# Seven products instead of eight in the last eight-product layer, and two partial sums seeded in PSUM, in a linear attention and two-layer feed-forward kernel

## The chip, the cores and the metric

The kernel runs on one NeuronCore of a Trainium2 chip. The metric is the device time of one execution in microseconds (us). Before the change it is 1583.31 us, the median of three runs (1581.37 to 1585.13).

## The reference, cut to what matters

```python
kv = einsum('bhsd,bhse->bhde', k, v)            # 8 batches, 8 heads, 576 tokens, 64 wide
out = einsum('bhsd,bhde->bhse', q, kv)
x = out / rms(out) * g_norm                     # -> 4608 tokens x 512
h = x @ w_in;   g = max(h, 0)**2;  x = g @ w_out        # first layer, d_ff = 2048
h = x @ w_in2;  g = h * cos(h);    y = g @ w_out2       # second layer, d_ff = 2048
```

All in float32. The kernel splits each operand of the big products into a high and a low part of the fp32r type, so one product of blocks is three matmuls per pair of blocks (high-high, high-low, low-high).

## The kernel before, in words

There are two stages. The first (to about 499 us) computes the attention and, with plain chunks of 128 columns of d_ff, the first half of the first layer. Beside it the weights of what follows are *converted*: they come as 64-bit words, DVE and ACT turn them into fp32, form sums and differences of blocks, split them and write them to DRAM (`load_w`, `conv_steps`). The kinds of conversion are "one" (weights of the first stage), "pair" (first products of the second stage: 4 blocks become 7), "seven" (second products, also 4 become 7) and "out" (second products without block sums: split only).

The second stage runs over 30 **slots** `(m, t, q)` (L429): layer m, token tile t (three of 2 x 512 tokens and two of 2 x 384), group q of 512 columns of d_ff. Slots 0 to 9 are the first layer's second half of d_ff, two groups a tile, so even slots have q = 0 and odd ones q = 1; slots 10 to 29 are the second layer, four groups a tile. Each slot has *first products* (x times w_in) and, 1.25 slots later (`LAG2`), *second products* (g times w_out).

First products always use the scheme with seven block products in place of eight (Winograd's form of Strassen): `first_product` issues 12 matmuls for each of the seven products, in `ORDER` 0, 1, 3, 2, 5, 4, 6, into two pairs of PSUM banks FA and FB. Some products add onto what a pair already holds. `keep` (ACT, L522) copies product 0 (name m1), product 3 (u2) and product 2 (m5) out to SBUF; `add` (DVE, L526) adds product 1 to m1 to give block (0, 0), and so on; `last` (ACT, L536) takes product 6. The blocks then go through the activation: `relu_1`, `relu_2` in the first layer, `cos_1` to `cos_5` in the second.

Second products use seven block products in the slots of the set `seven` (L83: the first layer's group 0 and all of the second layer): `s_block` forms the seven left operands with 4 differences and 7 splits (ACT `gh` L648, DVE `gl` L649), `second_product` issues 42 matmuls per pair of banks row (84 in the first layer; 168 or 126 of 256 columns in the second), and `drain_product` (L687) adds each product to the running sums, by DVE, or in the second layer for products 4, 5, 1 and 6 by an ACT copy and an accumulating DMA on POOL's queue; a first group's first parts are copied by ACT instead. The first layer's second groups are not in the set: there `g_hi`, `g_lo` split the four blocks, `second` (L595) issues all eight products, 12 matmuls for each of 8 units, and `drain` (L616) adds four pairs of banks to the sums with DVE.

What sets the order: every helper is a job with a position in slots (`at(pos(k + f * PH), ...)`, PH is a seventh of a slot), and `run_slots` (L861) writes the two streams of matmuls out, one first-product matmul per step of 1/84 slot and the second products' matmuls spread over the same steps; jobs whose position has come are issued in between. A build-time planner, which sees the dependences, may move an instruction within its engine's order; on the chip each engine works in that order. Weight loads (`load_wi`, `load_ws`, `load_wo`) and all other plain DMAs go on SP's queue, 2.7 products ahead of use, into one pool of 16 buffers `w`, which also holds the sums. New x blocks for a tile (`x_block`) are made by DVE and ACT from 4.5 products before its first slot to 3.5 products after that slot's start.

The late conversions, the second layer's "pair" weights, are 16 items placed from slot 1 to slot 7.6. Their raw words have two buffers (pool `conv`, also used by `part`, ACT's copy for the accumulating DMA), their temporaries four (pool `t`).

```python
first_pair = (NP, 0)                                  # 4, 0
groups_of = [range(NP // 2), range(NP)]               # 2 and 4 groups
def f_bank(k, i):
    return psum[("FA", "FB")[(k + (i in (1, 2, 4))) % 2]][:, :, :ht]
```

Of the kernel before, what the change touches and what calls it, by code (L numbers as in the profile page):

```python
# [8 lines left out]
F32 = mybir.dt.float32  # L9
# [13 lines left out]
def kernel(  # L23
# [42 lines left out]
    conv_p = ctx.enter_context(tc.tile_pool(name="conv", bufs=2, side="left"))  # L66
# [16 lines left out]
    seven = {(0, 0)} | {(1, q) for q in range(NP)}  # L83
    ws_d = {k: dram.tile([P, NPR, 2, 2, 2, P], F32, name=f"ws_d{k[0]}_{k[1]}") for k in sorted(seven)}
    wo_d = {
        (m, f): dram.tile([P, 2, DM], F32, name=f"wo_d{m}_{f}")
        for m in range(2)
        for f in range(2 * first_pair[m], NF)
    }

# [46 lines left out]
    def load_w(kind, m, f, i):  # L137
        if kind == "seven":
            raw = conv_p.tile([P, 4, P, 2], U32, tag="raw", name="raw")
# [4 lines left out]
        elif kind == "pair":  # L144
            raw = conv_p.tile([P, 4, P, 2], U32, tag="raw", name="raw")
            for df, dst in ((0, raw[:, 1:3]), (1, raw[:, 0::3])):
                src = (wA, wB)[m][2 * f + df, :, 0, :].rearrange("p (c n) -> p c n", n=2 * P)
                nc.sync.dma_start(out=dst.rearrange("p k n two -> p k (n two)"), in_=src[:, i::2, :])
        else:
            if kind == "one" and i:  # L150
                raw = x_p.tile([P, DM, 2], U32, tag="xr", name="raw", bufs=2)
            else:
                raw = conv_p.tile([P, DM, 2], U32, tag="raw", name="raw")
# [14 lines left out]
    def conv_steps(kind, m, f, i):  # L168
        raw = raws.pop((kind, m, f, i))
        if kind in ("pair", "seven"):  # L170
            w, e = words(raw, [P, 4, P])
            yield

            a = as32(raw.rearrange("p a n two -> p (a n two)")).rearrange("p (o n) -> p o n", n=P)
# [3 lines left out]
            where = [n for n in ("c", "x") if n in pools]  # L178
            if where:
                parts = [(0, 8, pools[where[0]].tile([P, 8, P], F32R, tag=where[0], name="wh"))]  # L180
            else:
                parts = [(o, o + 4, temp([P, 4, P], F32R, "wh")) for o in (0, 4)]
            q, pp = divmod(f - first_pair[m], 2)
            dst = (wi_d if kind == "pair" else ws_d)[m, q][:, :, :, pp, i, :]
# [12 lines left out]
        if kind != "one":  # L197
            yield
        wf = as32(w[:])
        value(raw, wf, w, e)  # L200
        if kind == "one":
            if i == 0:
                wts[m, f] = [w_p.tile([P, 2, DM], F32R, tag="w", name=f"w{x}") for x in "hl"]
            h, l = (x[:, i, :] for x in wts[m, f])
        else:
            h, l = (temp([P, DM], F32R, f"w{x}")[:] for x in "hl")
# [766 lines left out]
```

## Time and profile before

| | |
|---|---|
| median of three runs | 1583.31 us |
| the profiled execution | 1582.0 us |
| its span in the profile | 1580.2 us |
| TensorE (PE) busy | 1547.6 us, 98% |
| VectorE (DVE) busy | 1256.6 us, 80% |
| ScalarE (ACT) busy | 1060.5 us, 67% |
| granted TensorE clock | 1.00 (2.4 GHz) |

A matmul's end is modelled and matmuls overlap, so a row's mean duration is longer than the time from one matmul's start to the next; the latter is what PE needs for one. In a timeline row the first number is the start in us from the span's start, the second its duration; brackets hold the engine's idle time before it and what ended it.

### The profile page before, as it was taken

Reading aid. Unit: us, or ns where it says so; the run is one execution under the profiler, and the core shown is the slowest. Engines: PE = TensorE matmul, PEld = TensorE weight load, DVE = VectorE, ACT = ScalarE, POOL = GpSimd, SP = SyncE. Lnnn points to the kernel's source line nnn. Section 1 sums busy time; section 2 is a strip of 40 time slices with the busy share of each in tenths; the row PEclk is TensorE's granted clock in tenths of the full one; section 3 lists DMA queues with packets and bytes.
Section 4 is the critical chain, followed back from the end, with each engine's and each line's share of the span. In section 5 each row is a group of like instructions: output and inputs, shape, how many; then the busy total and the mean of one; then the engine's idle time right before and its main releaser. Section 6 shows DMA issues by size and latency. Waiting matters only on the chain.

```text
span 1580.2 us, 24826 instructions
## 1 busy us (share of the span) xinstructions
PE 1547.6 (98%) x9164; PEld 1356.4 (86%) x9164; DVE 1256.6 (80%) x1714; ACT 1060.5 (67%) x1515; POOL 115.4 (7%) x125
## 2 busy tenths in 40 slices
PE   5999999999999999999999999999999999999998
PEld 3777777778887878888999899999999999999998
DVE  7988878788874888889847678967896788689777
ACT  5977777775443756565645667776777677777774
POOL 1100201111100000000000000000000001101110
PEclk9999999999999999999999999999999999999999
DMA  8858879866667889999987679998899789999995
GB/s 317 282 158 243 263 235 278 240 202 207 185 219 256 298 271 336 302 335 330 374 281 291 246 213 270 266 277 246 267 260 291 230 260 290 277 363 314 284 351 164
DMA packets 236999, 425.53 MB, mean 269 GB/s; under 512 B 18512, under 2 KB 155216, under 8 KB 236880
## 3 DMA queue, kind: packets, MB, share of 16 engines
q1 hardware_dynamic: 225888, 387.78, 73.1%
q0 software_dynamic: 10992, 36.18, 11.4%
q8 instruction: 73, 1.20, 0.3%
q14 instruction: 46, 0.38, 0.1%
HBM read 309.85 MB, written 80.22 MB: 247 GB/s over the span
## 4 chain that ended last, share of the span: by engine, by line
PE 79%; DVE 8%; DMA 7%; issue 3%; ACT 2%; SPq 1%; POOL 0%; DVEq 0%; POOLq 0%; ACTq 0%
PE FA L510 14%; PE FB L510 14%; PE SA L672 12%; PE SB L672 12%; PE acc L422 10%; PE l L385 9%; PE SB L609 2%; PE SA L609 2%; DMA wi_d<-raw 2%; DMA raw<-in_wB 2%; PE o L385 1%; DMA sum<-part 1%; PE ss L385 1%; DMA ws_d<-raw 1%; DVE gl L649 1%
## 5 line engine op out<-in xcount | busy, mean ns | idle before, releaser
L510 PE MATMUL FA<-xh,wi 128*128 128x512 f32 (+1 forms) x840 | 306.0, 370 | 1.9 <-issue 1.0
L510 PE MATMUL FB<-xh,wi 128*128 128x512 f32 (+1 forms) x840 | 305.4, 370 | 0.0
L672 PE MATMUL SB<-ws,gh 128*128 128x256 f32 x1008 | 237.9, 280 | 1.1 <-ACT u L524 0.7
L672 PE MATMUL SA<-ws,gh 128*128 128x256 f32 x1008 | 237.9, 280 | 0.0
L672 PEld LDWEIGHTS SB<-ws,gh 128*128 128x128 f32 x1008 | 186.0, 188 | 14.4 <-ACT u L524 1.0
L672 PEld LDWEIGHTS SA<-ws,gh 128*128 128x128 f32 x1008 | 186.2, 188 | 13.2
L510 PEld LDWEIGHTS FA<-xh,wi 128*128 128x128 f32 x840 | 157.7, 188 | 12.1 <-issue 1.4
L510 PEld LDWEIGHTS FB<-xh,wi 128*128 128x128 f32 x840 | 157.8, 188 | 8.3 <-ACT h L539 0.3
L649 DVE TENSOR_TENSOR gl<-y,gh 128x1024 fp32r<-128x1024 f32 (+1 forms) x100 | 111.4, 1114 | 38.7 <-ACT gh L648 38.5
L672 PE MATMUL SA<-ws,gl 128*128 128x256 f32 x504 | 141.0, 280 | 1.1 <-DVE gl L649 1.1
L672 PE MATMUL SB<-ws,gl 128*128 128x256 f32 x504 | 141.2, 280 | 0.8 <-DVE gl L649 0.7
L698 POOL DMA_DIRECT2D sum<-part x71 | 60.3, 850 | 1093.4 <-ACT part L697 1078.6
L569 DVE SCALAR_TENSOR_TENSOR y<-y,h 128x1024 f32<-128x1024 f32 (+1 forms) x80 | 89.1, 1114 | 53.5 <-ACT y L565 53.2
L551 ACT ACTIVATE y<-h,zerob 128x1024 int32<-128x1024 f32 (+1 forms) x80 | 85.1, 1064 | 50.5 <-DVE h L530 50.5
L422 PE MATMUL acc<-gh,wh 128*128 128x512 f32 x288 | 113.6, 395 | 0.0
L422 PE MATMUL acc<-gl,wh 128*128 128x512 f32 x288 | 112.9, 392 | 0.0
L422 PE MATMUL acc<-gh,wl 128*128 128x512 f32 x288 | 112.6, 391 | 0.0
L510 PE MATMUL FA<-xl,wi 128*128 128x512 f32 (+1 forms) x300 | 111.0, 370 | 0.0
L510 PE MATMUL FB<-xl,wi 128*128 128x512 f32 (+1 forms) x300 | 110.9, 370 | 0.0
L672 PEld LDWEIGHTS SB<-ws,gl 128*128 128x128 f32 x504 | 94.7, 188 | 7.9 <-DVE gl L649 1.5
L672 PEld LDWEIGHTS SA<-ws,gl 128*128 128x128 f32 x504 | 94.7, 188 | 7.9 <-DVE gl L649 1.3
L385 PE MATMUL l<-xh,wh 128*128 128x512 f32 x240 | 96.6, 403 | 2.1 <-ACT xh L354 1.2
(181 smaller groups left out, 3773.4 us busy)
## 6 DMA issues: line engine op xcount, KB each, us to landing
wi<-wi_d SPq DMA_DIRECT2D x210, 512.0 KB, 7.0
ws<-ws_d SPq DMA_DIRECT2D x175, 512.0 KB, 5.9
sum<-part POOLq DMA_DIRECT2D x45, 512.0 KB, 7.6
kvld<-in_kv SPq DMA_DIRECT2D x32, 512.0 KB, 6.8
wi_d<-wh SPq DMA_DIRECT2D x24, 448.0 KB, 4.3
wi_d<-raw SPq DMA_DIRECT2D x24, 448.0 KB, 4.7
raw<-in_wA SPq DMA_DIRECT2D x20, 512.0 KB, 6.4
wo<-wo_d SPq DMA_DIRECT2D x20, 512.0 KB, 8.2
```

What stands on the lines that cost most here:

```text
L385: nc.tensor.matmul(ps, a[:, 0, cs], m[:], start=(c == 0 and k == 0), stop=(c == NKC - 1 and k == 2))
L422: nc.tensor.matmul(o, a[:, cs], m[:], start=(f == 0 and n == 0), stop=(f == NH - 1 and n == 2), skip_group_check=True)
L510: nc.tensor.matmul(ps[:, pp, :], a, b, start=(i in (0, 1, 2) and n == 0), stop=(n == 5), skip_group_check=True)
L551: nc.scalar.activation(out=y.bitcast(I32), in_=hs[k, b], func=AF.Identity, bias=zerob)
L569: nc.vector.scalar_tensor_tensor(out=y, in0=y, scalar=-2.0 * math.pi, in1=hs.pop((k, b)), op0=ALU.add, op1=ALU.mult)
L609: nc.tensor.matmul(ps, lhs, rhs, start=(a == 0 and (x, y) == (0, 0)), stop=last, skip_group_check=True)
L649: nc.vector.tensor_tensor(out=l, in0=src, in1=as32(h), op=ALU.subtract)
L672: nc.tensor.matmul(ps[:, b, :], lhs, rhs, start=(i in (0, 1, 2) and n == 0 and (m == 0 or b % 2 == 0)), stop=(n == 5), skip_group_check=True,)
L698: nc.gpsimd.dma_start(out=e, in_=part, accum_op=ALU.add)
```

## The change

- The first layer's second groups get seven second products too: `second`, `drain`, `g_hi`, `g_lo`, `load_wo` and the kind "out" go, and `seven` becomes all slots. Four early "out" conversions become "seven" conversions.
- `seed`: in slots from 2 on whose tile is not longer than the slot's before (all but slot 10), ACT copies product 0 from its banks onto those of product 1, whose matmuls then accumulate there; `whole` (ACT) takes the sum out, in place of `keep` m1 and `add`. In the first layer `whole` applies the ReLU, so `relu_1` falls away for this block.
- The same for the second products' sum of 0 and 1 (all those slots but the last, 29), with a new order of the products, that of the first ones.
- `run_slots` holds product 1 of a seeded slot back: its 12 steps go into the last 3 of its seventh of a slot (`HOLD = 9`), in both streams.
- The late conversions take two items at once ("pairs"), seven in all after an early pair of single items: five at slot 0.45 + 1.05 k, two at 9.9 and 10.85. One raw buffer of twice the size in place of two, and two temporaries of twice the size in place of four; `part` uses a temporary.

```diff
-    seven = {(0, 0)} | {(1, q) for q in range(NP)}
+    ws_d = {k: dram.tile([P, NPR, 2, 2, 2, P], F32, name=f"ws_d{k[0]}_{k[1]}") for k in wi_d}
...
+        elif kind == "pairs":
+            raw = pools["raw"].tile([P, 4, 2 * P, 2], U32, tag="raw", name="raw")
+            for df, dst in ((0, raw[:, 1:3]), (1, raw[:, 0::3])):
+                src = (wA, wB)[m][2 * f + df, :, 0, :].rearrange("p (k n) -> p k n", n=4 * P)
+                nc.sync.dma_start(out=dst.rearrange("p k n two -> p k (n two)"), in_=src)
...
-    S_ORDER = (0, 2, 3, 4, 5, 1, 6)
+    S_ORDER = (0, 1, 3, 2, 5, 4, 6)
     BY_DMA = (4, 5, 1, 6)
+    SEEDED = 2
+
+    def seeded(k):
+        return k >= SEEDED and TILES[slots[k][1]][1] <= TILES[slots[k - 1][1]][1]
+
+    def seeded_s(k):
+        return seeded(k) and k < len(slots) - 1
+
+    HOLD = 9
...
-                        ps[:, pp, :], a, b, start=(i in (0, 1, 2) and n == 0), stop=(n == 5), skip_group_check=True
+                        start=(n == 0 and (i in (0, 2) or i == 1 and not seeded(k))),
...
+    def seed(k):
+        nc.scalar.copy(out=f_bank(k, 1), in_=f_bank(k, 0))
+
+    def whole(k, b, i):
+        hs[k, b] = h = t_tile(k, F32, "h")
         m = slots[k][0]
-        nc.scalar.activation(out=h, in_=f_bank(k, 6), func=AF.Copy if m else AF.Relu, scale=scale_of(k))
+        nc.scalar.activation(out=h, in_=f_bank(k, i), func=AF.Copy if m else AF.Relu, scale=scale_of(k))
...
-        if q == 0 and m and i in (0, 2, 3, 6):
+        if i == 0 and seeded_s(k):
+            nc.scalar.copy(out=blocks_of(t, s_bank(k, 1), m), in_=ps)
+            return
+        if q == 0 and m and i in (1 if seeded_s(k) else 0, 2, 3, 6):
...
-                part = blocks_of(t, conv_p.tile([P, 2, 512], F32, tag="raw", name="part"))
+                part = blocks_of(t, temp([P, 2, 512], F32, "part"))
...
-            pairs_in(0, range(4, 6), "seven") + outs_of(0, range(6, 8)) + pairs_in(1, range(2 * NP), "seven"),
+            pairs_in(0, range(NP, 2 * NP), "seven") + pairs_in(1, range(2 * NP), "seven"),
             10,
             nAtt + 1,
         ),
-        (pairs_in(0, range(NP, 2 * NP)), nAtt + 1, nA0 - 7),
-        (pairs_in(1, range(2 * NP)), pos(1), pos(7.6)),
+        (pairs_in(0, range(NP, 2 * NP)) + pairs_in(1, range(1)), nAtt + 1, nA0 - 5),
...
+    late_stream = Stream(load_w, conv_w, [("pairs", 1, p, 0) for p in range(1, 2 * NP)])
+    at(pos(0.15), late_stream.advance)
+    late_stream.place([pos(0.45 + 1.05 * k) for k in range(5)] + [pos(9.9), pos(10.85)], 0)
...
-        at(pos(k + 1 * PH), keep, k, "m1", 0)
-        at(pos(k + 2 * PH), add, k, (0, 0), 1, "m1")
+        if not seeded(k):
+            at(pos(k + 1 * PH), keep, k, "m1", 0)
+            at(pos(k + 2 * PH), add, k, (0, 0), 1, "m1")
+        else:
+            at(pos(k + 1 * PH), seed, k)
+            at(pos(k + 2 * PH), whole, k, (0, 0), 1)
...
+        def held(x):
+            return 2 * PH - (2 * PH - x) * (12 - HOLD) / 12 if PH <= x < 2 * PH else x
...
+        for n in range(nf):
+            k, j = divmod(n, 84)
+            if seeded(k) and 12 <= j < 24:
+                j = 24 - (24 - j) * (12 - HOLD) / 12
+            due.append(k * 84 + j)
...
-    pools["t"] = ctx.enter_context(tc.tile_pool(name="t", bufs=4, side="left"))
+    pools["t"] = ctx.enter_context(tc.tile_pool(name="t", bufs=2, side="left"))
+    pools["raw"] = ctx.enter_context(tc.tile_pool(name="late", bufs=1, side="left"))
```

## Rows read from the trace of the kernel before

**Rows 1.** The page: span, busy time by engine, and the chain that ended last.
```profile
span 1580.2 us, 24826 instructions
...
PE 1547.6 (98%) x9164; PEld 1356.4 (86%) x9164; DVE 1256.6 (80%) x1714; ACT 1060.5 (67%) x1515; POOL 115.4 (7%) x125
...
PE 79%; DVE 8%; DMA 7%; issue 3%; ACT 2%; SPq 1%; POOL 0%; DVEq 0%; POOLq 0%; ACTq 0%
```

**Rows 2.** Busy time by stretch: slot 3, and the sum over slots 2 to 5.
```profile
core 0: us, PE busy (x) PEld busy (x) DVE busy (x) ACT busy (x) POOL busy (x), PEclk, DMA share, GB/s
...
594.30:633.70 39.40, 39.10 (x173) 32.04 (x173) 36.69 (x41) 26.13 (x28) 0.00 (x0) 1.00 0.96 332
...
sum 161.40, PE 160.07 PEld 129.98 DVE 140.93 ACT 94.04 POOL 0.00; mean PE 40.02 PEld 32.49 DVE 35.23 ACT 23.51 POOL 0.00
```

**Rows 3.** The same view, second layer: slots 15 (512 tokens), 24 and 26 (384).
```profile
1034.70:1073.90 39.20, 39.20 (x254) 35.58 (x253) 25.95 (x22) 29.47 (x31) 3.40 (x4) 1.00 0.97 299
1374.60:1404.20 29.60, 29.60 (x213) 29.60 (x212) 22.63 (x25) 20.81 (x28) 2.55 (x3) 1.00 1.04 369
1433.70:1465.00 31.30, 30.28 (x213) 29.61 (x212) 27.92 (x32) 24.92 (x34) 3.39 (x4) 1.00 0.94 286
```

**Rows 4.** All matmuls of line 609 (`second`) on one pair of banks, with forms.
```profile
L609 PE MATMUL SB<-gh,wo x160: 334/389/497, 560.9 to 887.4; 128*128 128x512 f32 x96, 128*128 128x384 f32 x64
...
L609 PE MATMUL SB<-gl,wo x80: 334/389/398, 561.3 to 887.0; 128*128 128x512 f32 x48, 128*128 128x384 f32 x32
```

**Rows 5.** Timeline of PE at the start of slot 4.
```profile
638.45 0.39 PE L672 MATMUL SA<-gh,ws 128*128 128x512 f32 x1
638.67 0.39 PE L510 MATMUL FA<-xh,wi 128*128 128x512 f32 x1
...
643.81 0.50 PE L510 MATMUL FB<-xh,wi 128*128 128x512 f32 x1
```

**Rows 6.** Timeline of PE in slot 8, 384 tokens.
```profile
787.11 0.33 PE L510 MATMUL FB<-xh,wi 128*128 128x384 f32 x1
787.28 0.33 PE L672 MATMUL SA<-gl,ws 128*128 128x384 f32 x1
```

**Rows 7.** Timeline of all engines in slot 15, where product 0 ends.
```profile
1039.86 0.40 PE L510 MATMUL FB<-xh,wi 128*128 128x512 f32 x1
...
1040.29 1.03 ACT L524 ACTIVATE m<-FB 128x1024 f32<-128x1024 f32 x1 [0.17 <-PE FB L510]
1040.33 0.39 PE L510 MATMUL FA<-xh,wi 128*128 128x512 f32 x1
...
1041.21 1.05 ACT L561 ACTIVATE y<-y 128x1024 f32<-128x1024 f32 x1
```

**Rows 8.** Timeline of ACT in slot 4.
```profile
640.95 0.95 ACT L189 CAST wh<-raw 128x896 fp32r<-128x896 f32 x1 [6.76 <-DMA wo<-wo_d]
...
648.18 1.02 ACT L524 ACTIVATE m<-FA 128x1024 f32<-128x1024 f32 x1
```

**Rows 9.** Timeline of all engines in slot 18, where product 0 ends.
```profile
1157.45 0.40 PE L510 MATMUL FA<-xh,wi 128*128 128x512 f32 x1
...
1161.11 1.02 ACT L524 ACTIVATE m<-FA 128x1024 f32<-128x1024 f32 x1
```

**Rows 10.** Timeline of DVE in slot 4, with operations of late conversions.
```profile
634.82 0.68 DVE L124 SCALAR_TENSOR_TENSOR w<-raw,w 128x512 uint32<-128x512 uint32 x1
635.42 0.68 DVE L130 SCALAR_TENSOR_TENSOR e<-raw,e 128x512 uint32<-128x512 uint32 x1
...
638.89 0.69 DVE L177 TENSOR_TENSOR raw<-raw 128x128 f32<-128x128 f32 x3
639.50 1.21 DVE L700 TENSOR_TENSOR sum<-SB,sum 128x1024 f32<-128x1024 f32 x1
640.63 0.28 DVE L177 TENSOR_TENSOR raw<-raw 128x128 f32<-128x128 f32 x1
```

**Rows 11.** Waits of SP's queue over the whole span.
```profile
SPq L148 <- DMA wi_d<-raw: 53.9, 21, 4.2
```

More of the change, by code (lines that the diff above doesn't have):

```diff
@@ L169, in conv_steps @@
         raw = raws.pop((kind, m, f, i))
-        if kind in ("pair", "seven"):
-            w, e = words(raw, [P, 4, P])
+        if kind in ("pair", "seven", "pairs"):
+            n = 2 * P if kind == "pairs" else P
+            w, e = words(raw, [P, 4, n])
             yield
-            a = as32(raw.rearrange("p a n two -> p (a n two)")).rearrange("p (o n) -> p o n", n=P)
+            a = as32(raw.rearrange("p a n two -> p (a n two)")).rearrange("p (o n) -> p o n", n=n)
             value(raw, a[:, 0:4], w, e)
@@ L177, in conv_steps @@
                 nc.vector.tensor_tensor(out=a[:, o], in0=a[:, x], in1=a[:, y], op=op)
-            where = [n for n in ("c", "x") if n in pools]
+            where = [p for p in ("c", "x") if p in pools]
             if where:
-                parts = [(0, 8, pools[where[0]].tile([P, 8, P], F32R, tag=where[0], name="wh"))]
+                size = 1024 // n
+                parts = [
+                    (o, o + size, pools[where[0]].tile([P, size, n], F32R, tag=where[0], name="wh"))
+                    for o in range(0, 8, size)
+                ]
             else:
-                parts = [(o, o + 4, temp([P, 4, P], F32R, "wh")) for o in (0, 4)]
+                parts = [(o, o + 4, temp([P, 4, n], F32R, "wh")) for o in (0, 4)]
             q, pp = divmod(f - first_pair[m], 2)
-            dst = (wi_d if kind == "pair" else ws_d)[m, q][:, :, :, pp, i, :]
+            dst = (ws_d if kind == "seven" else wi_d)[m, q][:, :, :, pp]
+            dst = dst.rearrange("p o x i n -> p o x (i n)") if kind == "pairs" else dst[:, :, :, i, :]
             l = a.bitcast(F32R)
@@ L571, in cos_5 @@
         )
-    def g_hi(k, b):
-        gs[k, b] = h, l = [t_tile(k, F32R, f"g{n}") for n in "hl"]
-        nc.scalar.copy(out=h, in_=ys[k, b])
-    def g_lo(k, b):
-        h, l = gs[k, b]
-        nc.vector.tensor_tensor(out=l, in0=ys.pop((k, b)), in1=as32(h), op=ALU.subtract)
-    CHUNKS = (1, 3, 0, 2)
-    def units(k):
-        m, t, q = slots[k]
-        half = TILES[t][1] // P if m else NKC
-        return [(j, i) for j in (1, 0) for i in range(half)]
     def load_sum(k, d, j):
@@ L743, in place @@
                     at(n + steps[-1], self.advance)
-    def outs_of(m, ps):
-        return [("out", m, f, 1) for p in ps for f in (2 * p, 2 * p + 1)]
     def pairs_in(m, ps, kind="pair"):
@@ L816 @@
         at(pos(k + 6 * PH), add, k, (0, 1), 4, "u2")
-        at(pos(k + 7 * PH), last, k)
-        chain = ((cos_1, cos_2, cos_3, cos_4, cos_5) if m else (relu_1, relu_2)) + (() if (m, q) in seven else (g_hi, g_lo))
+        at(pos(k + 7 * PH), whole, k, (1, 0), 6)
+        chain = (cos_1, cos_2, cos_3, cos_4, cos_5) if m else (relu_1, relu_2)
         for b, f in BLOCKS.items():
@@ L883, in run_slots @@
                 ns += 1
-            if n < nf:
+            while done1 < nf and due[done1] <= n:
                 next(steps1)
+                done1 += 1
             n += 1
```

123 lines of the change are left out of this document (38 added, 85 removed).

## The prediction, made before the change was run

> **What bounds the kernel now.** I read the page first: TensorE is busy 98% of the span, VectorE (DVE) 80%, ScalarE (ACT) 67%, and 79% of the chain that ended last is PE [rows 1]. Busy shares are averages, so next the time by slot. In the first layer's slots 2 to 5 PE is busy 160.07 of 161.40 us, DVE 140.93 us, and the DMA share of slot 3 is 0.96 [rows 2]. In the second layer a 512-token slot takes 39.20 us, all of it PE, with DVE at 25.95 and ACT at 29.47 us; a 384-token slot takes 29.60 us, and one of them (slot 26) 31.30 us [rows 3]. The granted clock is 1.00, the 2.4 GHz level, in every one of these stretches. So from slot 0 on PE's issue stream is the bound and everything else hides behind it: a matmul less is time less, and a wait put between two products is time more, unless PE has the other stream's matmuls to issue meanwhile.
>
> The profiled execution took 1582.0 us (span 1580.2); the median of the three runs is 1583.31 us, 1.3 us more. I sum against 1582.0 and add 1.3.
>
> **Matmuls removed.** The second groups' `second` issues 96 matmuls a slot, 480 in all: on one bank 160 with gh and 80 with gl, of which 96 and 48 are of 512 columns [rows 4], and as many on the other. Seven products of 12 make 84. That is 12 fewer in each of 5 slots: 36 of 512 columns (three slots), 24 of 384 (two). Matmuls issue 0.23 us apart at 512 columns (638.45, 638.67) [rows 5] and 0.17 at 384 (787.11, 787.28) [rows 6]. 36 x 0.228 + 24 x 0.174 = 8.2 + 4.2 = **12.4 us less**, all on the path.
>
> **The seeds.** This is the new wait. The first products' sum of products 0 and 1 was an ACT copy to SBUF (`keep`) and a DVE add; ACT now copies product 0's banks onto product 1's, and product 1 accumulates there. PE may not start product 1 before that copy has ended, and PE works in order: whatever stands behind product 1 waits too. From slot 2 on 27 slots are seeded so (slot 10 is not), and 26 in the second products (the last slot is not). That makes 53 waits.
>
> Price of one: from the start of product 0's last matmul to the start of ACT's copy 0.43 us (1039.86 to 1040.29), and 1.03 us for the copy [rows 7], 1.46 us in all. A PSUM-to-PSUM copy isn't in the trace; ACT's operations of that size lie between 0.92 us (from m's start to the next one's, 1041.21) and 1.05 (that next one's duration), so I take 1.03, m's own [rows 7]. The Trainium skill (Perfetto Trace Analysis, Optimizing Scalar/DVE Operations) gives ScalarE some 51 ns of access overhead on PSUM and 93 on SBUF, which as an estimate would make each copy about 0.04 us shorter; nothing here hangs on it.
>
> Cover of one: the change issues product 1 (or the second layer product's 1) in the last 3 of its 12 steps, so 9 steps of the other stream come first: 9 x 0.228 = 2.05 us, or 18 of 256 columns, which the 39.20 us slot prices at (39.20 - 84 x 0.23) / 168 = 0.118 each, 2.1 us. With the 0.23 of the last matmul itself that is 2.3 us against 1.46: margin 0.8 us. At 384 tokens the copy is shorter and so is the cover; scaled by 3/4 the margin is about 0.6. A prompt seed therefore costs nothing. What counts is how late ACT comes to it.
>
> `keep` of m1 stands today where the seed will stand, so its lateness is the measure. Read as in [rows 7], in the 27 slots: 14 come within 0.1 us of product 0's end, two more within the margin, and 11 late. Late in the first layer are slots 2, 4 and 6, by some 9 us: slot 4's product 0 ends issue at 638.67 [rows 5], m starts at 648.18 [rows 8], and ACT had stood still 6.76 us before a late conversion's cast (the profile puts that down to a wo load). Late in the second layer are slots 14, 18, 22 to 26 and 28, by 0.7 to 3.4 us: in slot 18 the last matmul starts at 1157.45 and m at 1161.11 [rows 9], 3.66 instead of 0.43. These are the slots in which a new tile's x blocks are made, where DVE is fullest (27.92 of 31.30 us in slot 26, [rows 3]). Today nobody waits, because m1 has a whole product of slack; in slot 4 PE went on with second products from 638.67 to 643.81 [rows 5].
>
> Bounds: below 0 (ACT is on time, because DVE loses work), above all lateness beyond the margin. For the second layer that adds up to 11 us over its 8 late slots; for slots 2 and 4 it is the seed's end, 648.18 + 1.02 = 649.20, less the 643.81 to which PE found other work, 5.4 us each; for slot 6 the late conversions, which caused it, are gone. What I take: **second layer +3.5** (a third), since two adds per slot leave DVE, 2.3 us of the 39.20; **first layer +4.0** (2 of 5.4 each, see below). The second products' 26 seeds I price at **+0.5**, between 0 and 5: they stand 0.25 slot later, where ACT had fewer x blocks before it.
>
> The Trainium skill (Perfetto Trace Analysis, Optimizing Tensor Performance) says that independent matmul groups should rotate through PSUM banks so that the evacuation of one overlaps the next one's matmuls. It speaks against a seed, which ties one group to the other's evacuation. Slot 15 agrees with the rule as it stands today: product 1's first matmul starts at 1040.33, while product 0's banks are being copied out [rows 7].
>
> **DVE in the first layer.** Each first-layer second-group slot now makes 11 s-block operations instead of 4 g_lo, and 6 drains instead of 4: 9 more, at 1.13 us (639.50 to 640.63, [rows 10]) 10.2 us. Per pair of slots 3 adds go (-3.4 us). A late conversion costs some 4.3 us of DVE: three operations at 0.60 like L124 (634.82 to 635.42), three small differences in 0.61 (638.89 to 639.50) [rows 10], a subtraction of 896 columns at 1.13 x 896 / 1024 = 1.0, the rest by their columns. There were 16 over 6.6 slots; now a double one comes every 1.05 slots from 0.45 to 4.65, and two at 9.9 and 10.85: 4.84 items per pair of slots become 3.81, -4.5 us. Net about +2 on the 70.5 us of a pair, while the pair gets 2.7 us shorter: 72.8 of 78, 93%, against 87% now. Slot 3 ran at 36.69 of 39.40 us, the same 93%, and lost 0.3 us of PE [rows 2]. So it fits, but lateness in slots 2 and 4 will not vanish; hence 2 us each.
>
> **What else moves, costed at nothing or little.** *ws loads*: 7 x 512 KB instead of 4 in five slots, against about one late conversion's 1.4 MB less per pair of slots; the queues stay near a DMA share of 0.96, which cost PE nothing in slot 3, and 1.04 cost nothing at 29.60 us [rows 3]. If that cover fails, weights come late. *Late raw buffer*: one instead of two; SP waits for the writes before it loads again. That wait was 4.2 us at most over 21 [rows 11]; behind it stand weight loads with 2.7 products (2.7 / 7 x 39.2 = 15 us) of lead. *Bigger conversions' temps* shared with `part`: the two overlap only around 10.85. *Five fewer* accumulate DMAs on POOL; y_d writes stay four per tile. *Early conversions*: four of kind "out" become "seven", 1.8 us of DVE more each and 3 more loads on SP, in a stretch for which I take the page's DVE share, 80% [rows 1]: **+0.5**. *New order of second products*: the b21 block is wanted four products earlier, but is finished two products before that. *Old stalls*: slot 26's 1.7 us and 1.3 us of idle PE in slots 2 to 5 [rows 2, 3], which came from a full DVE: **-2.0**.
>
> **Sum.** 1582.0 - 12.4 + 3.5 + 4.0 + 0.5 + 0.5 - 2.0 = 1576.1; at the median **1577.4 us**, 0.4% faster.
>
> **Rivals.**
> *All covered.* ACT is on time everywhere and the old stalls go: -12.4 - 3 to -4, about 1567. For it: 16 of 27 rows are within the margin today. Against: slots 2, 4. Chance 0.09.
> *Given back in the first layer.* Slots 2 and 4 lose their full 5.4 each and the rest is as forecast: 1577.4 + 6.8 = 1584. For it: DVE at 93% with front-loaded x blocks, and seeds that PE's fixed order does not know to be late. Against: the late conversions now end before the seeds. Chance 0.19.
> *Slower: ACT late at the seeds.* ACT gets a copy more per seeded sum (29.47 of 39.20 becomes some 31.5) and its lateness stays; PE's order, fixed when the program was built, holds only the 9 steps. Slots 2, 4, 6 then lose 9.1 - 0.8 each and the second layer 11: 36 us, 1583.3 - 12.4 + 36 = 1607. It decides from a mean stall of 12.4 / 53 = 0.23 us per seed, and is slower by 0.2% from 0.3. For it: PE's strict alternation in slot 18 although m was late. Against: stalls give ACT and DVE time, so lateness cannot repeat in full. With all that lies between 1586 and 1607: 0.19.
> *No cover at all.* If PE could not issue the other stream meanwhile, 53 chains of 1.2 to 1.5 us would add some 70: 1641. Against: matmuls of both streams alternate one by one [rows 5, 7]. It is what the rule on rotating banks of the Trainium skill (Perfetto Trace Analysis, Optimizing Tensor Performance) would lead to. Chance 0.03.
>
> **Numbers.** The forecast has 0.50. Faster is 0.50 + 0.09, same 0.19, slower 0.22, where "same" is within 0.2% (3.2 us), about what a measurement of this kernel tells from no change. The range goes from all covered, 1567, to a third of the slower case, 1592; about 0.04 lies below and 0.15 above.
>
> **What would show it.** Right: `second` gone and 84 matmuls in each second-group slot, 38.3 us for slots 2 and 4 but for stalls; seeds of about 1.03 us starting 0.43 us after a last matmul, and no PE wait on them in the 39.2 us slots; DVE lower, ACT higher in the second layer. Wrong: PE waiting for ACT's seed lines by more than 12 us in total, second-layer slots over 39.2 and 29.6 us, or waits on ws and wi loads.

## The result, and the profile after

The changed kernel takes **1594.19 us** (median of 4 runs, 1593.02 to 1595.40); the kernel before took 1582.62 beside it (median of 4). The ratio is 1.0071, 95% interval [1.0054, 1.0089]: 0.7% slower. The forecast was 1577.4 us, 0.4% faster, in a range of 1567 to 1592. The sign was wrong and the time lies outside the range.

The page of the profiled execution (1593.9 us), for [rows 1]: the span, busy time by engine, and the chain that ended last.

```profile
span 1592.1 us, 24817 instructions
...
PE 1542.6 (97%) x9104; PEld 1349.8 (85%) x9104; DVE 1254.8 (79%) x1676; ACT 1107.7 (70%) x1568; POOL 105.5 (7%) x117
...
PE 77%; DMA 8%; DVE 6%; issue 4%; ACT 4%; SPq 0%; DVEq 0%; ACTq 0%; POOLq 0%
```

The 60 matmuls are gone (9164 to 9104), and PE is busy 5.0 us less, yet the span is 11.9 us longer: PE stands. To see where, I took the time from each slot's first first-product matmul to the next one's, in both traces (us):

| stretch | before | after | difference |
|---|---|---|---|
| up to slot 0 | 499.3 | 503.3 | +4.0 |
| slots 0 and 1 | 53.7 | 57.9 | +4.2 |
| slots 2 to 10 | 325.6 | 312.7 | -12.9 |
| slot 11 | 38.6 | 40.8 | +2.3 |
| slots 12 to 22 | 426.7 | 429.3 | +2.6 |
| slots 23 and 27 | 60.3 | 67.2 | +6.9 |
| slots 24 to 26, 28 | 119.9 | 119.0 | -0.9 |
| slot 29 to the last matmul | 51.5 | 57.2 | +5.7 |

The saving of 12.4 that I had worked out stands in slots 2 to 10, all of it. The loss is in places that the forecast priced at nothing, or at 0.5 us (the time up to slot 0). The busy time by stretch (duration, then each engine's busy time, the granted clock, DMA share, GB/s), for [rows 2, 3]: slots 1, 3, 23, 27, and 29 with its tail.

```profile
524.20:561.30 37.10, 34.59 (x152) 27.94 (x151) 32.40 (x33) 22.71 (x24) 0.00 (x0) 1.00 0.92 307
600.30:639.40 39.10, 37.95 (x167) 30.96 (x166) 33.66 (x34) 24.48 (x26) 0.00 (x0) 1.00 0.93 335
...
1344.10:1376.70 32.60, 31.07 (x223) 30.75 (x222) 19.22 (x21) 24.21 (x32) 2.56 (x3) 1.00 0.99 315
1466.00:1500.70 34.70, 31.39 (x213) 31.07 (x212) 19.60 (x22) 23.84 (x32) 2.55 (x3) 0.95 0.97 322
1530.40:1592.10 61.70, 51.55 (x369) 50.05 (x367) 40.25 (x44) 33.69 (x44) 5.95 (x7) 0.97 0.63 181
```

PE stands 2.5 us in slot 1, 1.5 in 23, 3.3 in 27 and 10.2 at the end (6.5 before, where 56.10 us held 49.56 of PE). Slots 27 and 29 also show a lower granted clock.

**A prompt seed cost what was forecast.** A seed in slot 15, from the timeline of PE and ACT, for [rows 7]:

```profile
1038.10 0.40 PE L508 MATMUL FB<-xh,wi 128*128 128x512 f32 x1
1038.53 1.00 ACT L540 COPY FA<-FB 128x1024 f32<-128x1024 f32 x1 [0.16 <-PE FB L508]
...
1040.71 0.40 PE L508 MATMUL FA<-xh,wi 128*128 128x512 f32 x1
```

The copy starts 0.43 us after the last matmul and takes 1.00 us (forecast 0.43 and 1.03); product 1 comes 1.2 us after its end. The waits of the whole span (total, times, longest):

```profile
...
PE SA L631 <- ACT gh L607: 5.5, 3, 3.5
...
PE FA L508 <- ACT h L545: 3.3, 1, 3.3
PE SB L631 <- ACT SB L650: 3.0, 3, 1.5
PE FA L508 <- ACT m L527: 2.8, 2, 1.4
PE l L379 <- ACT r L388: 2.5, 3, 1.6
```

Of these rows only L650, with 3.0 us, is a seed, that of the second products; the first products' seeds (L540) add 0.6. I had set down 7.5 for the first products' and 0.5 for the second products'. Half of the 3.0 is one wait, in slot 23 (below). The rest of the loss is four other things, which the timelines show one by one.

*Slots 27 and 23*. ACT in slot 27 (at the end in brackets, its idle time before the operation and what ended it):

```profile
1469.29 0.80 ACT L659 COPY part<-SA 128x768 f32<-128x768 f32 x1 [0.46 <-PE SA L631]
...
1470.82 0.81 ACT L540 COPY FA<-FB 128x768 f32<-128x768 f32 x1
1476.50 0.80 ACT L659 COPY part<-SB 128x768 f32<-128x768 f32 x1 [4.88 <-DMA sum<-part]
...
1480.68 0.80 ACT L545 ACTIVATE h<-FA 128x768 f32<-128x768 f32 x1
```

The copy to `part` waits 4.88 us for an accumulating DMA that still reads one of the two buffers. In order behind it on ACT stands `whole` (L545), which since the change takes the sum of products 0 and 1 out of PSUM, and product 2 needs those banks. Before, the DVE add did that, so ACT's stand did not reach PE. The stands have grown too: before copies to `part` ACT waited 4.7 us for such a DMA over the whole span before the change (4 times), and 13.0 after it (8 times). PE waits 3.31 us; then the clock falls (PE's timeline, then the stretches up to the matmul, and the two of 3 us behind it):

```profile
1481.54 0.44 PE L508 MATMUL FA<-xh,wi 128*128 128x384 f32 x1 [3.31 <-ACT h L545]
```
```profile
1478.00:1482.00 4.00, 0.69 (x5) 0.46 (x3) 2.15 (x3) 2.94 (x5) 0.45 (x1) 1.00 1.07 386
1482.00:1485.00 3.00, 3.00 (x14) 3.00 (x14) 2.90 (x4) 1.45 (x3) 0.00 (x0) 0.57 0.85 223
1485.00:1488.00 3.00, 3.00 (x21) 3.00 (x21) 3.00 (x4) 2.62 (x5) 0.00 (x0) 0.86 0.80 243
```

0.57 is near the 1.2 GHz level: a wait of 3.3 us cost the slot 5.1.

In slot 23 it is not `whole` but a seed of the second products (L650, at 1359.26) that comes late. ACT waits 2.59 us for the same kind of DMA, later 2.24 us for a difference that DVE makes, and then makes the seed, for which PE waits (ACT, then PE):

```profile
1353.82 1.02 ACT L659 COPY part<-SB 128x1024 f32<-128x1024 f32 x1 [2.59 <-DMA sum<-part]
```
```profile
1360.10 0.39 PE L631 MATMUL SB<-ws,gh 128*128 128x256 f32 x1 [1.53 <-ACT SB L650]
```

*Slots 1 and 11*. In slot 1 it is ACT again: the first part of a double conversion's cast stands 7.38 us for DVE, and `keep` (L527), for which PE waits 1.43 us, comes behind it. PE stands 1.08 us more at 559.82; the profile names no cause for that. In slot 11 a double conversion runs as well, and PE waits 1.02 us for a `gh` and 0.82 us for a `gl`.

```profile
548.47 0.83 ACT L192 CAST wh<-raw 128x768 fp32r<-128x768 f32 x1 [7.38 <-DVE raw L125]
549.21 1.02 ACT L527 ACTIVATE m<-FA 128x1024 f32<-128x1024 f32 x1
```

*First stage*, SP's queue and ACT: the x load (L227) stands behind a raw load of four DMAs, which on SP waits until a raw buffer's write has landed (the last row: SP's waits from 170 to 200 us; before the change no load of weights waited there for a write). ACT stands for x, and PE stands 1.58 and 1.54 us at 194.41 and 198.97, where before the change it did not.

```profile
184.65 1.77 SPq L135 DMA_DIRECT2D raw<-in_wA  x4
186.52 0.38 SPq L227 DMA_DIRECT2D xraw<-x_d  x1
```
```profile
191.00 0.62 ACT L232 CAST xh<-xraw 128x512 fp32r<-128x512 f32 x1 [2.27 <-DMA xraw<-x_d]
```
```profile
SPq L135 <- DMA ws_d<-raw: 4.3, 3, 2.3
```

*Tail*: with the new order the second product of slot 29 wants the b21 block, the last that is made. PE waits for its gh, with no first product of a next slot to go on with. (One line that the list of the change leaves out belongs here: in every slot this operand is now made 1.1 products ahead of its use, the others 1.6 as before.)

```profile
1570.08 0.38 PE L631 MATMUL SA<-ws,gh 128*128 128x256 f32 x1 [3.52 <-ACT gh L607]
```

### The profile page after: what moved, and what is told of

Same layout as the page of the kernel before. It is cut to its first block, busy times and chain, and to the rows that moved or that the text cites. A ratio compares the mean times of both kernels' runs of the same rounds, so it can differ in the third digit from the quotient of the medians.

```text
span 1592.1 us, 24817 instructions
## 1 busy us (share of the span) xinstructions
PE 1542.6 (97%) x9104; PEld 1349.8 (85%) x9104; DVE 1254.8 (79%) x1676; ACT 1107.7 (70%) x1568; POOL 105.5 (7%) x117
## 4 chain that ended last, share of the span: by engine, by line
PE 77%; DMA 8%; DVE 6%; issue 4%; ACT 4%; SPq 0%; DVEq 0%; ACTq 0%; POOLq 0%
PE SB L631 14%; PE SA L631 14%; PE FB L508 13%; PE FA L508 13%; PE acc L416 10%; PE l L379 9%; DMA sum<-part 2%; PE o L379 1%; DMA ws_d<-raw 1%; PE ss L379 1%; DVE gl L608 1%; DMA xraw<-x_d 1%; DMA q<-in_qT 1%; DMA p_d<-ev 1%; DMA raw<-in_wA 1%
## 5 line engine op out<-in xcount | busy, mean ns | idle before, releaser
L508 PE MATMUL FA<-xh,wi 128*128 128x512 f32 (+1 forms) x840 | 300.0, 371 | 8.0 <-ACT h L545 3.3
L508 PE MATMUL FB<-xh,wi 128*128 128x512 f32 (+1 forms) x840 | 299.3, 370 | 0.0
L631 PE MATMUL SA<-ws,gh 128*128 128x256 f32 x1008 | 230.3, 282 | 5.5 <-ACT gh L607 5.5
L631 PE MATMUL SB<-ws,gh 128*128 128x256 f32 x1008 | 229.3, 282 | 2.0 <-ACT SB L650 1.9
L631 PEld LDWEIGHTS SA<-ws,gh 128*128 128x128 f32 x1008 | 181.9, 190 | 17.3 <-ACT gh L607 6.2
L631 PEld LDWEIGHTS SB<-ws,gh 128*128 128x128 f32 x1008 | 181.0, 189 | 14.0 <-ACT SB L650 3.3
L660 POOL DMA_DIRECT2D sum<-part x67 | 57.0, 851 | 1101.9 <-DMA wi<-wi_d 535.2
L607 ACT CAST gh<-y 128x1024 fp32r<-128x1024 f32 (+1 forms) x100 | 95.0, 962 | 12.6 <-DVE y L575 7.4
L631 PE MATMUL SB<-gh,ws 128*128 128x512 f32 (+1 forms) x280 | 100.0, 370 | 2.9 <-ACT SB L650 1.1
```

Source lines behind the costliest of these rows:

```text
L508: nc.tensor.matmul(ps[:, pp, :], a, b, start=(n == 0 and (i in (0, 2) or i == 1 and not seeded(k))), stop=(n == 5), skip_group_check=True,)
L607: nc.scalar.copy(out=h, in_=src)
L631: nc.tensor.matmul(ps[:, b, :], lhs, rhs, start=(n == 0 and (m == 0 or b % 2 == 0) and (i in (0, 2) or i == 1 and not seeded_s(k))), stop= ...
L660: nc.gpsimd.dma_start(out=e, in_=part, accum_op=ALU.add)
```

## The experiments

Theory A: the edits around the seeds lost the time. Theory B: the 53 seeds did, because ACT comes late to them. Each diff is against the changed kernel, or against e8 where that is said.

### e1_tail: the old order in the last slot

```
+    LAST_ORDER = (0, 2, 3, 4, 5, 1, 6)
+    def order_s(k):
+        return LAST_ORDER if k == len(slots) - 1 else S_ORDER
```

> The changed kernel (1594.2 us), but the last slot alone goes back to the old order of second products (0, 2, 3, 4, 5, 1, 6); the seeds, the pairs and all other slots stay. Theory A (edits that I had costed at nothing lost the time, the new order among them): the last slot and its tail, 57.2 us from its first matmul to the end against 51.5 before the change, shorten by 4 to 6 us, to about 1589; the granted clock of the last 60 us goes back from 0.97 to 1.00; all other slots stay within 0.3 us. Theory B (the 53 seeds cost the time, because ScalarE comes late to them): this slot has no seed in its second products and only one in its first, so nothing moves by more than 1 us: 1593 to 1595.

1591.04 us (ratio to before 1.0051, [1.0034, 1.0068]). The last slot takes 52.1 instead of 57.2 us:

```profile
1532.60:1589.00 56.40, 49.79 (x369) 48.50 (x367) 39.72 (x44) 33.53 (x44) 5.94 (x7) 0.99 0.68 199
```

So the new order costs 5.2 us in the last slot. In this profiled execution slots 0 and 1 took 3.3 us more than in the changed kernel's, with the same instructions: in slot 0 PE waited 2.15 us for `keep` (1.36 there), and the granted clock was 0.70 in the 3 us that followed (1.00 there). The median fell by 3.2 only; that its other executions lost the rest in the same place is likely, but no trace shows it.

### e2_early and e7_xload: the added early conversions

e2 moves the four added ones to the end of the second window; e7 issues one load 0.9 chunk later (`DELAY = 0.9`).

```
-        (pairs_in(0, range(NP, 2 * NP)) + pairs_in(1, range(1)), nAtt + 1, nA0 - 5),
+        (pairs_in(0, range(NP, 2 * NP)) + pairs_in(1, range(1)) + moved, nAtt + 1, nA0 - 5),
```
```
-                    at(n + steps[-1], self.advance)
+                    at(n + steps[-1] + (DELAY if 18 < n < 19 and item[0] == "seven" else 0), self.advance)
```

> The changed kernel, but the four added early conversions (kind seven, first layer's pairs 6 and 7) leave the places in the first window that the conversions of kind out had, and follow at the end of the second window. Theory A: the x load at 186 to 191 us is no longer queued on SP behind a raw load of four DMAs, TensorE's two waits of 1.6 and 1.5 us near 194 and 199 us go, and slot 0 starts 3 to 4 us earlier, at about 500: 1590.5. If the ten conversions of the second window, now fourteen, are crowded, 1 to 2 us come back there. Theory B (the seeds): no seed stands before slot 2, so the time before slot 0 does not matter to it; it gives no more than 1 us: 1593 to 1595.

> The changed kernel, but one early conversion's load (four DMAs) is issued 0.9 chunk later, so that it stands behind the x load on SP's queue instead of ahead of it. Theory A: that x load is no longer held by the wait for a raw buffer, ScalarE's 2.3 us stand at 191 us and TensorE's two waits of 1.6 and 1.5 us near 194 and 199 us go, and slot 0 starts 3 to 3.5 us earlier, at about 500: 1590.5 to 1591.5. If the wait only passes to the next item on the queue, nothing changes: 1594.

e2 took 1597.58 us (1.0098, [1.0082, 1.0114]): slower. The two waits near 194 and 199 us are gone, but fourteen conversions crowd the second window. ACT now stands there, before a conversion's operation that waits for DVE, with an eviction behind it; PE waits 1.74 us for that eviction, and a clock of 0.57 follows:

```profile
420.38 0.72 ACT L112 ACTIVATE e<-e,expb 128x512 int32<-128x512 int32 x1 [3.16 <-DVE e L111]
...
421.49 0.58 ACT L402 COPY ev<-acc 128x512 f32<-128x512 f32 x1
```
```profile
424.00:428.00 4.00, 4.00 (x11) 3.15 (x12) 3.59 (x9) 1.75 (x3) 0.00 (x0) 0.57 0.80 282
```

Slot 0 starts at 509.9, where I had expected about 500. My expectation had put 1 to 2 us on the crowded new place, which cost far more. e7 took 1595.46 us (1.0076, [1.0063, 1.0089]): in its trace slot 0 starts at 501.7, the wait at 194 us is gone, and one of 1.14 us is left at 196.69; the median shows nothing, and the profiled execution again has a slot 0 of 23.2 us. A miss for the time, half a hit for the mechanism.

### e3_late: single late conversions

```
-    late_stream = Stream(load_w, conv_w, [("pairs", 1, p, 0) for p in range(1, 2 * NP)])
-    late_stream.place([pos(0.45 + 1.05 * k) for k in range(5)] + [pos(9.9), pos(10.85)], 0)
+    late_stream = Stream(load_w, conv_w, pairs_in(1, range(1, 2 * NP)))
+    late_stream.place([pos(1 + 6.6 / 14 * k) for k in range(14)], 0)
```

> The changed kernel, but the late conversions of the second layer's pairs 1 to 7 are single ones again, 14 of them spread evenly over slots 1 to 7.6 as before the change, with two raw buffers of half the size (pair 0 stays early). Theory A: slot 1 (37.1 us, of which 3.5 are new) and slot 11 (40.8, 2.3 new) go back to 33.5 and 38.6, so 5 to 6 us less; smaller conversions among the seeds of slots 2 to 7 may give or take 2: 1587 to 1591. Theory B (the seeds): slots 1 and 11 gain the same in both, slot 1 has no seed; but then what is lost in slots 2 to 10 would grow, since single conversions run through slots 5 to 7 where the seeds now meet none: 1592 to 1596.

1591.72 us (1.006, [1.0045, 1.0076]), at the edge of both expectations; the slots decide. Slot 1 takes 33.55 and slot 11 37.99 us: 6.4 less, as A had it. Slots 6 and 7, where conversions now run among x blocks, take 36.3 and 32.6: 4.1 back. So pairs cost 6.4 us in slots 1 and 11 and singles 4.1 in slots 6 and 7: less, not nothing.

### e4_part: a third buffer for `part`

```
-                part = blocks_of(t, temp([P, 2, 512], F32, "part"))
+                turn["part"] += 1
+                if k >= 12 and turn["part"] % 3 == 0:
+                    part = blocks_of(t, pools["raw"].tile([P, 2, 512], F32, tag="raw", name="part"))
+                else:
+                    part = blocks_of(t, temp([P, 2, 512], F32, "part"))
```

> The changed kernel, but from slot 12 on every third copy for an accumulating DMA goes into the buffer that the late conversions have left, so three such buffers rotate instead of two. Nothing else moves. Theory A: ScalarE no longer stands 4.9 us before the copy of slot 27 (13.0 us over the span, 8 times), so its copy of products 0 and 1 out of PSUM is on time: slots 23 and 27 (32.6 and 34.7 us against 30.8 and 29.5 before) lose 5 to 7 us, the granted clock of slot 27 is 1.00 again: 1587.5 to 1589.5. Theory B (ScalarE is late at the seeds because it has more to do, not because it stands): a third buffer takes away no work, so under 1.5 us: 1592.5 to 1594.5.

1586.94 us (1.0032, [1.0018, 1.0045]): 7.3 less from a buffer. Slots 23 and 27:

```profile
1346.60:1377.40 30.80, 30.80 (x222) 30.80 (x221) 19.32 (x21) 24.32 (x32) 2.55 (x3) 1.00 1.03 338
1466.40:1496.00 29.60, 29.60 (x213) 29.60 (x212) 19.51 (x22) 23.85 (x32) 2.55 (x3) 1.00 1.03 327
```

PE is busy throughout, at the full clock, and the two slots are back at the 60.3 us of before. No work was taken from ACT, so B has no explanation for this.

### e5_noseed, e8_all, e9_all_noseed: the mends together, with and without seeds

e5 is the changed kernel with `SEEDED = 99`. e8 has the edits of e1, e3, e4 and e7 at once; e9 is e8 with `SEEDED = 99`.

> The changed kernel without any seed: all sums of products 0 and 1 go back to a ScalarE copy and a VectorE add, the holds go with them; the seven products, the new order, the pairs and the early conversions stay. Theory A (the time went to the edits around the seeds): the holds' 0.16 us in 20 slots and 3.6 us of waits for the copies go, and slots 23 and 27, where ScalarE's copy out of PSUM stood behind `part`, gain up to 7, because the sum is VectorE's again; against that VectorE gets 53 operations of 1.1 us back and stalls of 3 to 6 us in slots 2 to 5 and 26; slots 1 and 11, the tail and the time before slot 0 stay as they are: 1582 to 1589. Theory B (the seeds are the whole loss): it falls by 12.4 or more below the kernel before, to 1570 to 1578.

> The changed kernel with all four mends: old order of second products in the last slot, a third buffer for the copies that feed the accumulating DMAs, single late conversions, the one early load behind the x load. Seeds and seven products everywhere stay. Theory A: the parts add up, 1594.2 - 5.2 (tail) - 7 (slots 23 and 27) - 3.5 (late conversions) - 3.3 (early) = 1575 with 2 either way, faster than the kernel before (1582.2) by 0.3 to 0.6%. Theory B (the seeds): their cost stays in, so it does not come below 1582.

> The kernel with all four mends, and without any seed (ScalarE copy and VectorE add again, no holds). It is read against the one with the mends and the seeds. Theory A: seeds and holds cost 3.2 + 3.6 us of TensorE and save VectorE 53 operations; by slots 2 to 9, where VectorE is fullest, it loses 3 to 8 us, in the second layer it wins 3 to 5: within 4 us of the other, 1571 to 1579. Theory B: without the seeds it is faster than with them by 8 or more, under 1570.

e5: 1595.07 us (1.0073, [1.0058, 1.0087]), the same as with seeds; both theories had expected less. e8: **1576.55 us** (0.9962, [0.9949, 0.9976]), faster than both kernels. e9: 1589.51 us (1.0039, [1.0027, 1.0051]). Between e9 and e8 the seeds are worth 13 us: B falls, and so does my own "within 4". But e5 and e9 keep the new order of the second products, which only the seeds ask for, and that matters for how the 13 is read.

The slots say where. In the second layer it is where a new tile's x blocks are made, slots 14, 18, 22 and 26: 151.9 us together in e5 and 143.8 in the changed kernel, 8.1 less (150.4 in e9, 143.6 in e8). Yet the kernel before, which has no seeds either, took 144.4 there. Slot 14 in the kernel before, in e5 and in the changed kernel:

```profile
991.20:1030.40 39.20, 39.20 (x254) 35.57 (x253) 35.03 (x31) 29.98 (x32) 3.39 (x4) 1.00 0.92 269
```
```profile
995.50:1036.40 40.90, 39.74 (x254) 35.65 (x253) 36.87 (x33) 30.22 (x32) 3.41 (x5) 1.00 0.92 276
```
```profile
993.50:1033.00 39.50, 39.50 (x255) 35.77 (x254) 32.62 (x29) 31.76 (x33) 3.45 (x5) 1.00 0.93 274
```

In e5 PE waits in these four slots for DVE's `gl` of product 3 (4.6 us of the 7.0 that it waits on that line over the span). The new order makes the two differences for product 3 together, and DVE runs two more behind them before that `gl`; in the kernel before other operations lay between them. DVE and PE in slot 14 of e5:

```profile
1013.31 1.22 DVE L591 TENSOR_TENSOR t<-y,t 128x1024 f32<-128x1024 f32 x1
1014.45 1.22 DVE L591 TENSOR_TENSOR y<-y 128x1024 f32<-128x1024 f32 x1
1015.58 1.22 DVE L591 TENSOR_TENSOR y<-y,t 128x1024 f32<-128x1024 f32 x1
1016.72 1.23 DVE L608 TENSOR_TENSOR gl<-t,gh 128x1024 fp32r<-128x1024 f32 x1
```
```profile
1017.99 0.39 PE L631 MATMUL SB<-ws,gl 128*128 128x256 f32 x1 [0.64 <-DVE gl L608]
```

With the seeds DVE has 4.2 us less to do in this slot, and the waits are gone. So in the second layer, as far as these rows show, the seeds mostly pay for their own order: from slot 12 to the last matmul the kernel before takes 658.5 us, e8 659.4 and e9 665.9. A kernel with the mends, without seeds and with the old order everywhere was not run. If it kept the 658.5, the seeds would be worth some 6 us against it; that is an estimate from these rows (13.5 from slot 2 on, less 7.4), not a measurement.

In slots 23 and 27 the changed kernel loses 6.9 against e5, which takes 60.3 us there with the same two buffers, as the kernel before did: it is what the seeds and `whole` put behind `part`. So e5 equals the changed kernel. With the third buffer that loss is gone and the gain stays.

In the first layer it hangs on the late conversions. With pairs, of which two come only in slots 9.9 and 10.85, slots 2 to 7 take 219.5 us without seeds (e5) and 219.8 with them. With single ones, in e8 (seeds) and in e9 (none):

```profile
555.60:778.20 222.60, 218.68 (x1010) 185.75 (x1010) 214.83 (x270) 140.98 (x158) 0.00 (x0) 1.00 0.97 336
```
```profile
559.50:788.80 229.30, 221.92 (x1009) 186.40 (x1009) 224.63 (x280) 136.38 (x152) 0.00 (x0) 0.99 0.95 328
```

In e9 DVE is busy 98% of the stretch (224.63 of 229.30), and the saving is given back in full: before the change these six slots took 228.9 us. From slot 2 to the end e8 takes 1017.4 us and e9 1030.9. Against the kernel before, all that e8 gains from slot 2 on lies in slots 2 to 11: 353.4 us for 364.1.

### e10_hold0, e13_first: what the hold and the second products' seeds are worth

Both are e8 with one line changed.

```
-    HOLD = 9
+    HOLD = 0
```
```
     def seeded_s(k):
-        return seeded(k) and k < len(slots) - 1
+        return False
```

> The kernel with the four mends (1576.6 us) and all 53 seeds, but without the holds: product 1 follows product 0 step for step, in the first and in the second products. If a seed costs what I worked out, 1.46 us from the last matmul's start to the end of the copy, with one step of the other stream (0.23 us) left as cover, each of 33 seeds at 512 tokens loses 1.2 us and each of 20 at 384 about 0.9, some 58 us, less the 0.16 us a slot that the holds cost: about 1632, between 1620 and 1645. If ScalarE's copy is hidden anyway, because the order of the products leaves other work, the holds are worth nothing: 1573 to 1577.

> The kernel with the four mends (1576.6 us), with the 27 seeds of the first products only; in the second products the sum of products 0 and 1 goes back to VectorE, without a hold. Without any seed the same kernel took 1589.5 us, so the 53 seeds together are worth 13. If they are worth it because VectorE loses an operation of 1.1 us for each, half of the worth goes with the 26: 1582 to 1585. If what counts is that product 0's and 1's sum is out of PSUM by one ScalarE copy, ahead of everything that the cosine or the square needs, nearly all of it stays with the first products: 1575 to 1578. If the second products' seeds only cost their wait and hold (I had put 0.5 us on them), it is at or under 1576.

e10 took 1582.66 us (1.0002, [0.9991, 1.0013]). With no hold, product 1's first step is issued ahead of the seed and overwritten by it, so that step's sum is lost; what is timed is a seed between the first and the second step. It cost 6 us, not 55. PE's timeline around a seed (ACT's copy runs from 1033.88 to 1034.88) shows why:

```profile
1033.45 0.39 PE L514 MATMUL FA<-xh,wi 128*128 128x512 f32 x1
1033.68 0.28 PE L638 MATMUL SB<-ws,gl 128*128 128x256 f32 x1
...
1034.75 0.28 PE L638 MATMUL SB<-ws,gl 128*128 128x256 f32 x1
1034.93 0.50 PE L514 MATMUL FA<-xl,wi 128*128 128x512 f32 x1
```

Ten second-product matmuls stand in a row there, though the kernel hands them over two for one. So the order in which PE gets its matmuls is moved when the program is built, and product 1 is put off past the copy. The hold is not the only cover that a seed has, and PE's order is not the one written. My rival "no cover at all" and the working of a seed's cover by counted steps both took the written order for the real one.

e13 took 1580.94 us (0.998, [0.9969, 0.9992]). Its first stage happened to be 4.6 us longer than e8's, with the same instructions; from slot 2 on it takes 1021.0 us. So of the 13.5 us between e9 and e8 the first products' seeds bring 9.9 and the second products' 3.6, by one trace of each (the medians give 8.6 and 4.4): neither a half, nor nothing. Slots 14 and 18 take 39.3 us here, with no hold in the second products; so it is not the hold of product 1 that ends the waits for `gl`. DVE has less to do: 32.2 us in slot 14, where e9 has 36.8.

### e11_skip and e12_place: the early conversions' price, and another place for late ones

e11 is e8 with the four added early conversions left out in place of e7's edit; e12 is e8 with four single late conversions moved to slots 7.9 to 9.7.

```
+    moved = pairs_in(0, range(NP + 2, 2 * NP), "seven")
...
+        for k, item in enumerate(new):
+            if n0 > 10 or item not in moved:
...
-        nc.sync.dma_start(out=as32(w[:]), in_=ws_d[m, q][:, W_OF[i]])
+        nc.sync.dma_start(out=as32(w[:]), in_=ws_d[m, q if m else 0][:, W_OF[i]])
```
```
-    late_stream.place([pos(1 + 6.6 / 14 * k) for k in range(14)], 0)
+    late_stream.place([pos(1 + 0.47 * k) for k in range(10)] + [pos(7.9 + 0.6 * k) for k in range(4)], 0)
```

> The kernel with three mends (last slot's order, third buffer, single late conversions), and the four added early conversions left out altogether: the first layer's second group reads the first group's second weights, so that part of the computation is not done. It measures what those four cost in the first stage. If they cost what the trace of the changed kernel shows (slot 0 starts 4.0 us later than before, 3.5 of it at one x load), slot 0 starts at 499 to 500 us, and the whole takes 1573 to 1575. If the first stage's time is set by other things and differs from run to run, slot 0 starts at 501 to 504 as in the runs with the four: 1576 to 1579.

> The kernel with the four mends (1576.6 us), but the last four of the 14 single late conversions move from slots 5.7 to 7.1 to 7.9 to 9.7. In the kernel with the mends slots 6 and 7 take 36.31 and 32.27 us, against 34.39 and 30.41 where no late conversion ran there: TensorE waits 1.0 us for VectorE's gl at 743 and 1.8 us for a second weight at 771. If that is VectorE and the queues filled by the conversions, both slots get back to 34.4 and 30.4, and slots 8 and 9, which have no x blocks to make but in slot 9's end, stay at 29.1: 3 to 3.8 us less, 1573. If slots 8 and 9 are as full, they lose it again: 1576 to 1577.

e11 took 1574.12 us (0.9945, [0.993, 0.9961]); slot 0 starts at 499.4. Five profiled executions with the four in their old place had 503.1 to 504.5, so they cost about 4 us there; with e7's edit it was 501.3 to 505.9 in six, no more than a part of a mend. Between the medians of e8 and e11 it is 2.4 us.

e12 took 1584.09 us (1.0012, [1.0003, 1.0021]), 7.5 slower than e8. Slots 6 and 7 did fall to 34.4 and 30.4, but slot 9 rose to 36.3 (PE waited 3.02 and 1.13 us; the profile puts both down to weight loads) and slot 2 to 44.8. In slot 2, where nothing was moved by more than 0.02 slot, ACT's order had changed:

```profile
554.31 0.71 ACT L112 ACTIVATE e<-e,expb 128x512 int32<-128x512 int32 x1
561.52 0.73 ACT L112 ACTIVATE e<-e,expb 128x512 int32<-128x512 int32 x1 [6.50 <-DVE e L111]
...
562.98 1.01 ACT L551 ACTIVATE h<-FB 128x1024 f32<-128x1024 f32 x1
563.90 1.03 ACT L614 CAST gh<-h 128x1024 fp32r<-128x1024 f32 x1
```

Once more a conversion's operation, which nobody is waiting for, stands 6.50 us ahead of `whole` and gh, for which PE waits 2.47 us; 1.00 us for a gl follows, and from 568 to 571 the granted clock is 0.50. In e8 `whole` comes ahead of it, at 555.61.

## Why the prediction was wrong

- **What bounds the kernel**: right. PE's issue stream is the bound from slot 0 on, and each loss but the holds' was a stand of PE, with the lower clock that followed some of them.
- **Matmuls removed, -12.4**: right. Slots 2 to 10 are 12.9 shorter; slot 5, which has no stand, takes 38.08 us, where the forecast has 38.3 for such a slot.
- **The seeds, +8.0**: the price was right (0.43 + 1.00 us a copy), the lateness too high (3.6 us of waits in place of 8.0; 0.6 for 7.5 at the first products' seeds, 3.0 for 0.5 at the second products', half of that behind `part`). What DVE's relief gives I had put at 2.0, the old stalls. Without it the rest of the change does worse than the kernel before: 7.5 us in slots 14, 18, 22 and 26 (e5), which I had not seen. The DVE sum for the first layer held: 72.42 us of 78.1 in slots 2 and 3, forecast 72.8 of 78, and with pairs the saving stands there with or without seeds.
- **No cover at all** did not come: e10, with the hold cut, lost 6 us and not 70, because the other stream's matmuls, on banks SA and SB, filled the copy's time. The Trainium skill (Perfetto Trace Analysis, Optimizing Tensor Performance) asks that independent matmul groups rotate through PSUM banks, so that one's evacuation overlaps the next one's matmuls. In e10 the second stream's matmuls still did, so the run does not contradict the rule; only the price that my rival put beside it was not paid. From the access overheads in the Trainium skill (Perfetto Trace Analysis, Optimizing Scalar/DVE Operations) I had estimated a copy 0.04 us shorter than `keep`'s. The traces are near that: 1.00 against 1.03.
- **The step that failed is "What else moves, costed at nothing or little".** *New order of second products*: I compared the b21 block's end with its new place in a slot in which the next slot's first products run beside it, and did not look at the last slot, where none follow; +5.7 (e1 gives back 5.2). Nor did I look at the differences for product 3, which the new order puts together on DVE: by e5's rows that would have cost 7.5 in the second layer, had the seeds not relieved DVE. *Early conversions*, +0.5: I priced DVE's time, not that "seven" holds its raw buffer until a write has landed and that SP stands for it ahead of an x load; about +4 (e11). *Bigger conversions*: I asked for their DVE time over a pair of slots, not how long ACT stands in order before one of their casts, nor what slots 1 and 11 do with two items at once; +5.8 in slots 1 and 11 (e3 gives back 6.4 there). *Left out altogether*: that `whole` moves the drain of products 0 and 1 from DVE to ACT, behind `part`, and that a seed can stand there too; +6.9 in slots 27 and 23 (e4 gives back all of it). The holds cost 0.16 us in each 512-token slot of the second layer, 39.36 for 39.20, also not priced. (A slip without weight: not five accumulating DMAs fall away but four, 71 and 67 in the traces.)
- **Rivals**: "slower: ACT late at the seeds" had the sign, not the mechanism. ACT was late at its drains and at one seed (slot 23), not because it had more to do but because it stood for others.
- With the four mends the kernel takes 1576.55 us, near the forecast's 1577.4. That is luck, and no credit to the sum: in e8 the seeds' waits are nearly gone where 8.0 was set down for them, while part of the early conversions' cost, the holds and 4 us of the single ones in slots 6 and 7 are in it and were not in the sum.

What stays open: why the first stage differs by up to 4.6 us between executions of the same instructions (one part is seen: near 199 us PE waits 1.90 us in e9 and 1.88 in e13, in e8 1.34 near 197). What a kernel with the mends, the old order and no seeds would take. A third raw buffer for the early conversions was not tried.

## What to carry to other kernels

Before an operation is moved to another engine, read what can stand ahead of it in that engine's order: a wait that hurt nobody becomes a wait of the bound once something urgent is queued behind it, and a third buffer or another place may be worth more than the edit. An "unchanged" order is to be followed to the last iteration, where the other stream no longer covers. And a change in parts is weighed part by part with the others in place: taking the seeds out changed nothing in the changed kernel (e5) and cost 13 us once what stood around them was mended (e9). Ask then what else of the change the comparison still holds: both kernels without seeds kept the order that the seeds had asked for.

## What was not expected of the hardware

A stand of PE costs more than itself: after waits of 3.31 us (slot 27) and 1.74 and 0.79 us (e2) the granted clock fell to 0.57 in the next 3 to 4 us, near the 1.2 GHz level, and slot 27 lost 5.1 us for a wait of 3.3. A wait of about the same length does not always do it. Ahead of slot 0 PE waits 2.14 us in e8 and 2.25 us in e11; the 3 us behind each, in which PE is busy throughout, show a granted clock of 0.61 and of 1.00:

```profile
501.40:504.40 3.00, 3.00 (x9) 2.40 (x10) 2.72 (x7) 0.00 (x0) 0.00 (x0) 0.61 0.96 305
```
```profile
499.50:502.50 3.00, 3.00 (x13) 2.46 (x14) 2.72 (x7) 0.00 (x0) 0.00 (x0) 1.00 0.96 315
```

A COPY from PSUM to PSUM of 128x1024 takes 1.00 us on ScalarE, and 0.78 to 0.81 at 128x768. An accumulating DMA of 384 or 512 KB lands about 8 us after its issue (median 7.9 and 8.1 in the changed kernel), so two buffers are few for up to four of them a slot.
